# Two full sets of second-weight buffers, four staging buffers and no resident token operands in an attention and mixture-of-experts kernel

## The chip, the cores and the metric

The kernel runs on one core of a Trainium2 chip. The metric is the device time of one execution in microseconds, the median of several runs. Engines are named as in the profile: PE is TensorE (its weight loads are PEld), DVE is VectorE, ACT is ScalarE, POOL is GpSimd, SP is SyncE, which issues all the transfers.

## What is computed

Linear attention with positive random features feeds a dense mixture of eight experts. The reference, cut to what matters:

```python
def _attn_ref(q, k, v, omega):                 # q, k, v: (4, 8, 576, 64), omega: (128, 64)
    def phi(x):
        h = np.einsum('bhsd,md->bhsm', x, omega) - np.sum(x * x, axis=-1, keepdims=True) / 2.0
        h = h - np.max(h, axis=-1, keepdims=True)
        return np.exp(h) / np.sqrt(m)
    q_p, k_p = phi(q_s), phi(k_s)
    kv = np.einsum('bhsm,bhsd->bhmd', k_p, v)
    ...
    return num / den
def _moe_ref(x, w_gate, w1, w2):               # x: (2304, 512), w1: (8, 512, 1024), w2: (8, 1024, 512)
    P = np.exp(x @ w_gate - max); 8 times: rows normalized, columns normalized
    for e in range(E):
        out += P[:, e:e + 1] * (np.maximum(x @ w1[e], 0.0) @ w2[e])
```

`x` is the attention's output, 2304 tokens of 512 features. The output is 2304 x 512 in float32.

## The kernel before

**Stages.** The attention part and the preparation of the token operands take about the first 219 us of the profile. Then the experts run in 16 units: a unit `u` is one expert and one half of its 1024 hidden columns (`units`, L172). In a unit, tokens go in three chunks of 768 (`NCH`) for the first layer and in nine pairs of 128-token tiles (`n` from 0 to 8, `steps`, L504) for the second.

**Seven products.** Each of the two layers is cut into 2 x 2 blocks and multiplied with seven products in place of eight; `ORDER = [1, 5, 6, 3, 7, 2, 4]` (L91) is the order in which they are taken. For that, sums of blocks are made of the weights (`split`, L187), of the tokens (`token_operands`, L97) and of the hidden activations (`left_operands_a` and `left_operands_b`, L593 and L609). Each float32 operand is cut into a high part (a rounding copy on ACT: `wh`, `ah`, `sh`, `bh`) and a low part (a subtraction on DVE: `wl`, `al`, `sl`, `bl`), and each product is high x high, high x low and low x high, so six matmuls of 256 columns in the second layer and two times six of 384 columns in the first.

**First layer.** `first(u, c, i, g)` (L527) multiplies token operand `i` of chunk `c` (tiles `xs`, or `xr`) by first weight `i` into `hx` or `hz`; DVE and ACT gather it in `hr` and `hn`. The first layer runs one chunk ahead of the second: the list `todo` is taken up five, five and four pieces a pair.

**Second layer.** `second(s, i)` (L630) multiplies a left operand by second weight `i` in a bank `x`, `z` or `w`, and DVE adds the result, times the token's weight `prob`, to the output tile (`out`, L660). A bank takes the next product only after that eviction.

**Weights of the next unit.** `stage(u, w)` (L176) loads first (`w` = 1) or second (`w` = 2) weights in two halves into staging tiles `st`. `split(u, w, i)` makes operand `i` from them: a combining step on POOL (in place in `st`, or in `t`) for 5, 6, 7 and 4 of the second weights and for 5, 6, 3 and 7 of the first, the high part on ACT, the low part on DVE (L193, L223, L224).

- There are three staging buffers, so the second half of the second weights has to wait until a half of the first weights is used up.
- First weights have 7 buffers for each part, second weights 7 + `W2X` = 11: four products of the next unit can be made while the present set is in use. In the code they stand ahead of pairs 4 to 7; the other three follow the last uses in pair 8.

**Token operands.** The 21 operands (three chunks of seven, 768 KB each) are in DRAM (`xd`). Operand 1 of each chunk (`RES = (1,)`) is loaded once and stays in a tile `xr`. The other six of a chunk are loaded again in each unit into four rotating buffers (`XSB`); `load_next` (L513) loads the next one when an operand has been used.

**What sets the order.** The code gives an order and priorities; a scheduler then places the instructions of each engine in a queue by its own estimate of when operands and buffers are ready, and it may move an instruction far ahead of its place in the code. Each engine takes its queue strictly in order. SP's queue holds the staging loads and the token loads together, so a load there waits behind one whose buffer is not free.

```python
pool = wp if w == 1 else op_
bufs = 7 + W2X * (w == 2)
hi = pool.tile([P, 2, HD], F32R, tag=f"w{w}h", bufs=bufs, name="wh")
lo = pool.tile([P, 2, HD], F32R, tag=f"w{w}l", bufs=bufs, name="wl")
nc.scalar.copy(hi, o)
```

Of the kernel before, what the change touches and what calls it, by code (L numbers as in the profile page):

```python
# [9 lines left out]
F32 = mybir.dt.float32  # L10
# [6 lines left out]
def raw(ap):  # L17

    return ap.bitcast(F32)
# [3 lines left out]
def moe_attention_kernel(  # L23
# [29 lines left out]
    P = 128  # L53
# [3 lines left out]
    SM = JM * P  # L57
    SR = S - SM
    XSB = 4
    RES = (1,)  # L60
    W2X = 4
    FB = 4
    NFB = FF // P // FB
    CT = 6
# [3 lines left out]
    HD = DM // 2  # L68
# [5 lines left out]
    wp = ctx.enter_context(tc.tile_pool(name="wp", bufs=1, side="right"))  # L74
# [14 lines left out]


    ORDER = [1, 5, 6, 3, 7, 2, 4]  # L91
    xdram = {}

    def token_tile():
# [2 lines left out]
    def token_operands(c, x):  # L97
# [11 lines left out]

        for i in ORDER:  # L110
            if i == 5:
# [61 lines left out]
    wst, wt = {}, {}  # L173
    tmp = {}

    def stage(u, w):  # L176
        e, fb = units[u]
        f0 = fb * FB * P
        for r in range(2):
            wst[u, w, r] = t = wp.tile([P, 2, 2, HD], F32, tag="st", bufs=3, name="st")  # L180
            if w == 1:
                src = w1[e][r * HD : (r + 1) * HD, f0 : f0 + FB * P]
            else:
                src = w2[e][f0 + r * HD : f0 + (r + 1) * HD, :]
            nc.sync.dma_start(out=t.rearrange("p k h c -> p k (h c)"), in_=src.rearrange("(k p) c -> p k c", p=P))

    def split(u, w, i):  # L187

        def q(r, h):
            return wst[u, w, r][:, :, 1 - h if w == 1 else h]  # L190

        def tt(o, a, b, op=ALU.subtract):
            nc.gpsimd.tensor_tensor(o, a, b, op=op)  # L193


        if w == 1:

            if i == 5:
                tmp[u] = wp.tile([P, 2, HD], F32, tag="t", bufs=1, name="t")
                tt(tmp[u], q(0, 1), q(1, 1), ALU.add)  # L200
            elif i == 6:
                tt(tmp[u], tmp[u], q(0, 0))
            elif i == 3:
                tt(tmp[u], q(1, 0), tmp[u])
            elif i == 7:
                tt(q(0, 1), q(0, 0), q(0, 1))
            o = {1: q(0, 0), 7: q(0, 1), 2: q(1, 0), 4: q(1, 1)}[i] if i not in (5, 6, 3) else tmp[u]
        else:

            if i == 5:  # L210
                tt(q(0, 0), q(0, 1), q(0, 0))
            elif i == 6:
                tt(q(0, 0), q(0, 0), q(1, 1))
            elif i == 7:
                tt(q(0, 1), q(1, 1), q(0, 1))
            elif i == 4:
                tt(q(0, 0), q(1, 0), q(0, 0), ALU.add)
            o = {3: q(1, 1), 7: q(0, 1), 2: q(1, 0)}.get(i, q(0, 0))
        pool = wp if w == 1 else op_
        bufs = 7 + W2X * (w == 2)  # L220
        hi = pool.tile([P, 2, HD], F32R, tag=f"w{w}h", bufs=bufs, name="wh")
        lo = pool.tile([P, 2, HD], F32R, tag=f"w{w}l", bufs=bufs, name="wl")
        nc.scalar.copy(hi, o)  # L223
        (nc.vector if u > 0 or (w == 2 and i in (1, 6, 7, 4)) else nc.gpsimd).tensor_tensor(lo, o, raw(hi), op=ALU.subtract)  # L224
        wt[u, w, i] = (hi, lo)
# [18 lines left out]
    for i in range(2):  # L244
        r, cl = slice(i * D, (i + 1) * D), slice(i * M, (i + 1) * M)
# [257 lines left out]
    NP = CT // 2 * NCH  # L503
    steps = [(u, n) for u in range(len(units)) for n in range(NP)]  # L504
    def order(u):

        return [NCH - 1] + list(range(NCH - 1)) if u == 0 else list(range(NCH))

    chunks = [(u, c) for u in range(len(units)) for c in order(u)]
    hraw, hneg, ops, xop, xres, hacc = {}, {}, {}, {}, {}, {}  # L510
    loads = [(u, c, i) for u, c in chunks[1:] for i in ORDER]

    def load_next():  # L513

        while loads:
            u, c, i = loads.pop(0)
            if i in RES:
                if (c, i) not in xres:
                    xres[c, i] = op_.tile([P, 2, 2, HL], F32R, name=f"xr{c}_{i}")
                    nc.sync.dma_start(out=raw(xres[c, i]), in_=xdram[c, i])  # L520
                xop[u, c, i] = xres[c, i]
                continue
            xop[u, c, i] = token_tile()
            nc.sync.dma_start(out=raw(xop[u, c, i]), in_=xdram[c, i])
            return

    def first(u, c, i, g):  # L527
# [38 lines left out]
        if g == 1 or both is None:  # L566
# [5 lines left out]
            else:  # L572
                nc.scalar.copy(o, src)  # L573
        if g == 1 and (u, c) != chunks[0] and i not in RES:
            load_next()

    def tiles_of(u, n):

        c, j = order(u)[n // (CT // 2)], n % (CT // 2)
        return [CT * c + j, CT * c + j + CT // 2]  # L580
# [81 lines left out]
    def store(t):  # L662
        b, j = t // JM, t % JM
        if b < B:
            dst = out[b * S : b * S + SM, :].rearrange("(p j) d -> p j d", j=JM)[:, j, :]
            nc.sync.dma_start(out=dst, in_=outt[t])
        else:
            for a in range(2):
                r0 = (2 * j + a) * S + SM
                nc.sync.dma_start(out=out[r0 : r0 + SR, :], in_=outt[t][a * SR : (a + 1) * SR, :])  # L670

    pieces = [(u, c, i, g) for u, c in chunks for i in ORDER for g in range(2)]

# [56 lines left out]
    for i, jb in enumerate(jobs):  # L730
# [4 lines left out]
        if i >= 8 and i % 2 == 0 and (i - 8) // 2 < 7:  # L735
            split(0, 1, ORDER[(i - 8) // 2])
        if i == 24:
# [20 lines left out]
    for _ in range(XSB):  # L758
        load_next()
    for i in ORDER:  # L760
        split(0, 2, i)
# [3 lines left out]
    for s, (u, n) in enumerate(steps):  # L765
        c = n // (CT // 2)
        more = u + 1 < len(units)
        if u == NFB:
            for t in tiles_of(u, n):
                nc.vector.tensor_scalar_mul(outt[t], outt[t], prob[:, t, 0:1])  # L770
        if more:
            if n == 1:
                stage(u + 1, 1)
            if n == 2:
                split(u + 1, 1, ORDER[0])
            if n == NP - 2 - W2X:
                stage(u + 1, 2)
            if NP - 1 - W2X <= n < NP - 1:
                split(u + 1, 2, ORDER[n - (NP - 1 - W2X)])
        for k, i in enumerate(ORDER):  # L780
            second(s, i)
            if n == NP - 1 and more and k + W2X < len(ORDER):
                split(u + 1, 2, ORDER[k + W2X])
            if k < (5, 5, 4)[n % 3] and todo:
                pc = todo.pop(0)
                first(*pc)
                j = ORDER.index(pc[2])
                if pc[1] == order(pc[0])[-1] and pc[3] == 1 and pc[0] + 1 < len(units) and j + 1 < len(ORDER):
                    split(pc[0] + 1, 1, ORDER[j + 1])
            if i == 7 and s + 1 < len(steps):  # L790
                left_operands_a(s + 1)
            if k in (1, 4):
                next(gate, None)
        if s + 1 < len(steps):
            left_operands_b(s + 1)
        if s == NFB * NP - 1:
            for _ in gate:
                pass
        if u == len(units) - 1:
            for t in tiles_of(u, n):  # L800
                store(t)
        ops.pop(s)
# [28 lines left out]
```

## Time and profile before

| | |
|---|---|
| median of 3 runs | 1668.83 us (1668.63 to 1671.46) |
| profiled execution | 1676.44 us, span 1674.7 us |
| PE busy | 1626.8 us, 97% |
| PEld busy | 1601.4 us, 96% |
| DVE busy | 1430.5 us, 85% |
| ACT busy | 783.6 us, 47% |
| POOL busy | 250.1 us, 15% |
| DMA | 293.19 MB in the main queue, 53.0% of 16 engines |

A profile is one execution seen by engine. Busy time is the union of an engine's instructions. Matmuls are pipelined and overlap in the list, so the distance from one start to the next says what a matmul costs when nothing holds it. "Idle before" is the time in which an engine did nothing, and the arrow names what ended it. The chain of waits is followed back from the last instruction, at each step to what released it.

### The profile page before, as it was taken

To read this page: it belongs to the slowest core of one execution; us is meant where nothing else is said; L and a number is where in the kernel's file an instruction comes from. 1 tells how busy PE (TensorE), PEld (TensorE's weight loads), DVE (VectorE), ACT (ScalarE), POOL (GpSimd) and SP (SyncE) were. 2 spreads that over 40 slices of the span, in tenths; PEclk is the share of its full clock that TensorE was granted. 3 is DMA by queue.
4 is the path that set the end of the run, shared out by engine and by line. 5 is a ranking of instruction groups with operands and counts; after the bars stand their busy time and mean duration, and the time that the engine had idled before them with its cause. 6 is when DMAs were issued, how large, how long until landed. Compare 5 with 4: busy or idle time off the path is not lost.

```text
span 1674.7 us, 29917 instructions
## 1 busy us (share of the span) xinstructions
PE 1626.8 (97%) x11610; PEld 1601.4 (96%) x11610; DVE 1430.5 (85%) x2903; ACT 783.6 (47%) x1408; POOL 250.1 (15%) x232
## 2 busy tenths in 40 slices
PE   7999989999999999999999999999999999999998
PEld 7899889999999999999999999999999999999997
DVE  7999788898978888898888887888889888888878
ACT  6777645443344344443444443434444344444432
POOL 7531131110111011010101010101101010101000
PEclk9999999999999999999999999999999999999999
DMA  9422575554554555556555454555564654555452
GB/s 242 119 80 99 218 284 190 196 194 159 169 177 159 195 175 176 195 162 209 177 175 188 163 187 163 176 189 183 166 206 157 205 185 162 189 159 194 159 189 76
DMA packets 96347, 295.08 MB, mean 176 GB/s; under 512 B 13776, under 2 KB 38352, under 8 KB 96208
## 3 DMA queue, kind: packets, MB, share of 16 engines
q1 hardware_dynamic: 96208, 293.19, 53.0%
q8 instruction: 92, 1.51, 0.4%
q14 instruction: 47, 0.39, 0.1%
HBM read 271.93 MB, written 21.23 MB: 175 GB/s over the span
## 4 chain that ended last, share of the span: by engine, by line
PE 73%; DVE 16%; DMA 5%; issue 2%; ACT 2%; POOL 1%; SPq 0%; ACTq 0%; DVEq 0%
PE hx L554 20%; PE x L640 19%; PE hz L554 13%; PE z L640 10%; DMA st<-in_moe_w_dram 5%; PE w L640 5%; DVE sm L591 3%; DVE wl L224 2%; DVE out L660 2%; DVE hr L571 1%; PE np L433 1%; DVE mx L347 1%; POOL st L193 1%; ACT wh L223 1%; DVE bl L591 1%
## 5 line engine op out<-in xcount | busy, mean ns | idle before, releaser
L554 PE MATMUL hx<-xs,wh 128*128 128x384 f32 x1160 | 279.9, 336 | 0.8 <-ACT hr L573 0.5
L554 PE MATMUL hz<-xs,wh 128*128 128x384 f32 x1152 | 278.3, 336 | 0.0
L660 DVE SCALAR_TENSOR_TENSOR out<-x,prob,out 128x256 f32<-128x256 f32 x504 | 237.8, 476 | 22.9 <-PE x L640 22.8
L554 PEld LDWEIGHTS hx<-xs,wh 128*128 128x128 f32 x1160 | 204.1, 188 | 1.4 <-ACT hr L573 0.9
L554 PEld LDWEIGHTS hz<-xs,wh 128*128 128x128 f32 x1152 | 203.2, 188 | 0.1
L622 ACT ACTIVATE bh<-hr 128x512 fp32r<-128x512 f32 x144 | 91.1, 633 | 233.0 <-PE x L640 188.1
L223 ACT CAST wh<-st 128x512 fp32r<-128x512 f32 x176 | 106.7, 618 | 194.9 <-POOL st L193 80.1
L224 DVE TENSOR_TENSOR wl<-st,wh 128x512 fp32r<-128x512 f32 x169 | 135.1, 802 | 67.2 <-ACT wh L223 66.3
L660 DVE SCALAR_TENSOR_TENSOR out<-z,prob,out 128x256 f32<-128x256 f32 x252 | 120.1, 476 | 83.2 <-PE z L640 83.0
L591 DVE SCALAR_TENSOR_TENSOR sm<-hr,sm 128x256 f32<-128x256 f32 x288 | 147.8, 513 | 3.9
L554 PE MATMUL hx<-xs,wl 128*128 128x384 f32 x580 | 150.8, 336 | 0.0
L554 PE MATMUL hz<-xs,wl 128*128 128x384 f32 x576 | 149.7, 335 | 0.0
L193 POOL TENSOR_TENSOR st<-st 128x512 f32<-128x512 f32 x80 | 106.7, 1342 | 231.1 <-DMA st<-in_moe_w_dram 177.0
L618 ACT CAST sh<-sm 128x512 fp32r<-128x512 f32 x144 | 89.6, 622 | 99.7 <-PE z L640 75.6
L640 PE MATMUL z<-wh,sh 128*128 128x256 f32 x576 | 117.4, 284 | 13.0 <-DVE out L660 12.2
L640 PE MATMUL x<-wh,sh 128*128 128x256 f32 x576 | 118.9, 288 | 2.7 <-ACT wh L223 1.3
L640 PE MATMUL z<-wl,sh 128*128 128x256 f32 x576 | 119.6, 282 | 0.8 <-POOL wl L224 0.8
L640 PE MATMUL x<-wl,sh 128*128 128x256 f32 x576 | 117.0, 281 | 0.0
L640 PE MATMUL z<-wh,sl 128*128 128x256 f32 x576 | 115.1, 281 | 1.8 <-DVE sl L606 1.8
L640 PE MATMUL x<-wh,sl 128*128 128x256 f32 x576 | 115.4, 281 | 0.0
L591 DVE SCALAR_TENSOR_TENSOR bl<-hr,bh 128x512 fp32r<-128x512 f32 x144 | 112.9, 784 | 0.0
L193 POOL TENSOR_TENSOR t<-st 128x512 f32<-128x512 f32 x16 | 21.2, 1322 | 608.4 <-DMA st<-in_moe_w_dram 527.3
(153 smaller groups left out, 3968.4 us busy)
## 6 DMA issues: line engine op xcount, KB each, us to landing
xs<-xd SPq DMA_DIRECT2D x282, 768.0 KB, 4.4
st<-in_moe_w_dram SPq DMA_DIRECT2D x64, 512.0 KB, 5.7
xd<-xs SPq DMA_DIRECT2D x21, 768.0 KB, 4.2
k<-in_k_dram SPq DMA_DIRECT2D x8, 512.0 KB, 6.7
v<-in_v_dram SPq DMA_DIRECT2D x8, 512.0 KB, 5.6
q<-in_q_dram SPq DMA_DIRECT2D x8, 512.0 KB, 6.5
out_dram<-out SPq DMA_DIRECT2D x16, 256.0 KB, 2.3
xr<-xd SPq DMA_DIRECT2D x3, 768.0 KB, 11.5
```

What stands on the lines that cost most here:

```text
L193: nc.gpsimd.tensor_tensor(o, a, b, op=op)
L223: nc.scalar.copy(hi, o)
L224: (nc.vector if u > 0 or (w == 2 and i in (1, 6, 7, 4)) else nc.gpsimd).tensor_tensor(lo, o, raw(hi), op=ALU.subtract)
L347: nc.vector.reduce_max(mx, p3, axis=AX.X)
L433: nc.tensor.matmul(n3[:, i, :], lhsT=qt[g][:, i, :], rhs=kvs[key[0]][:, h, :], start=True, stop=True)
L554: nc.tensor.matmul(pb, lhsT=a[:, k, g * P : (g + 1) * P], rhs=x[:, b, k, :], start=i in (1, 5, 2) and j == 0, stop=j == len(prods) - 1, sk ...
L571: nc.vector.tensor_tensor(o, src, o, op=ALU.add)
L591: nc.vector.scalar_tensor_tensor(o, in0=a, scalar=0.0, in1=b, op0=ALU.max, op1=op)
L618: nc.scalar.copy(sh, sm)
L622: nc.scalar.activation(bh, a[:, 1:], AF.Relu)
L640: nc.tensor.matmul(pb, lhsT=ops[s][i][a][:, f], rhs=wt[u, 2, i][b][:, f], start=bool(start) and j == 0, stop=j == len(prods) - 1, skip_gro ...
L660: nc.vector.scalar_tensor_tensor(o, in0=pb, scalar=prob[:, t, e : e + 1], in1=o, op0=ALU.mult, op1=ALU.add)
```

## The change

```diff
-    RES = (1,)
-    W2X = 4
+    RES = ()
...
+    W2AT = [(5, 2), (6, 0), (6, 3), (7, 0), (7, 3), (8, 0), (8, 3)]
...
-            wst[u, w, r] = t = wp.tile([P, 2, 2, HD], F32, tag="st", bufs=3, name="st")
+            wst[u, w, r] = t = wp.tile([P, 2, 2, HD], F32, tag="st", bufs=4, name="st")
...
-        bufs = 7 + W2X * (w == 2)
+        bufs = 7 * w
...
-            if n == NP - 2 - W2X:
+            if n == 2:
                 stage(u + 1, 2)
-            if NP - 1 - W2X <= n < NP - 1:
-                split(u + 1, 2, ORDER[n - (NP - 1 - W2X)])
         for k, i in enumerate(ORDER):
             second(s, i)
-            if n == NP - 1 and more and k + W2X < len(ORDER):
-                split(u + 1, 2, ORDER[k + W2X])
+            if more and (n, k) in W2AT:
+                split(u + 1, 2, ORDER[W2AT.index((n, k))])
```

- Second weights have 14 buffers for each part, two full sets.
- Staging has four buffers. The second weights are staged in pair 2 of the code and not in pair 3.
- The seven splits of the second weights stand at seven places in pairs 5 to 8 (`W2AT`), behind product `k` of pair `n`.
- No token operand is resident: operand 1 of each chunk goes through the four rotating buffers too, so seven of seven are loaded in each unit.

In the changed kernel's listing, line numbers are one higher from L92 on to the changed loop.

**SP's queue in unit 9, pairs 4 to 7, before.** `xs` is a token load, its source `xd0_5` is operand 5 of chunk 0; `st_13184` is the second half of the second weights of unit 10.

```order
L524 DMA xs_13361<-xd0_5_1826 128x1536
L524 DMA xs_13395<-xd0_6_1908 128x1536
L185 DMA st_13184<-in_moe_w2_dram 128x2x512
L524 DMA xs_13472<-xd0_3_1986 128x1536
L524 DMA xs_13507<-xd0_7_2076 128x1536
```

The same place in the changed kernel; `st_14189` and `st_14191` are the two halves of the second weights of unit 11:

```order
L525 DMA xs_13409<-xd0_1_1733 128x1536
L525 DMA xs_13443<-xd0_5_1826 128x1536
L186 DMA st_14189<-in_moe_w2_dram 128x2x512
L525 DMA xs_13515<-xd0_6_1908 128x1536
L525 DMA xs_13554<-xd0_3_1986 128x1536
L186 DMA st_14191<-in_moe_w2_dram 128x2x512
L525 DMA xs_13635<-xd0_7_2076 128x1536
```

The staging of second weights stands one unit further ahead, and operand 1 of chunk 0 (`xd0_1`) is loaded like the others.

**DVE's queue where unit 9 ends and unit 10 begins, before.** `wl` is a low part of a weight, here of second weights of unit 10; `out` rows are evictions, `sm`, `al`, `bl`, `sl` belong to the left operands.

```order
L660 SCALAR_TENSOR_TENSOR out14_3431<-x_13783,prob_79,out14_3431 128x256
L591 SCALAR_TENSOR_TENSOR al_13868<-hr_13566,ah_13867 128x256
L224 TENSOR_TENSOR wl_13793<-st_13182,wh_13792 128x512
L591 SCALAR_TENSOR_TENSOR sm_13892<-hr_13566,sm_13871 128x256
L591 SCALAR_TENSOR_TENSOR sm_13892<-hr_13566,sm_13892 128x256
L660 SCALAR_TENSOR_TENSOR out16_3300<-x_13671,prob_79,out16_3300 128x256
L660 SCALAR_TENSOR_TENSOR out17_3432<-z_13803,prob_79,out17_3432 128x256
L591 SCALAR_TENSOR_TENSOR bl_13780<-hr_13195,bh_13779 128x512
L224 TENSOR_TENSOR wl_13812<-st_13184,wh_13811 128x512
L660 SCALAR_TENSOR_TENSOR out14_3431<-x_13783,prob_79,out14_3431 128x256
L224 TENSOR_TENSOR wl_13833<-st_13182,wh_13832 128x512
```

The changed kernel, some ten instructions later in the queue; the `wl` rows are four of the seven second weights of unit 11:

```order
L607 TENSOR_TENSOR sl_13927<-sm_13925,sh_13926 128x512
L592 SCALAR_TENSOR_TENSOR sm_14037<-hr_13613,hn_13885 128x512
L225 TENSOR_TENSOR wl_14723<-st_14189,wh_14722 128x512
L225 TENSOR_TENSOR wl_14793<-st_14191,wh_14792 128x512
L225 TENSOR_TENSOR wl_14844<-st_14189,wh_14843 128x512
L592 SCALAR_TENSOR_TENSOR sm_14058<-hr_13613,sm_14037 128x256
L225 TENSOR_TENSOR wl_14914<-st_14191,wh_14913 128x512
L592 SCALAR_TENSOR_TENSOR sm_14058<-hr_13613,sm_14058 128x256
L661 SCALAR_TENSOR_TENSOR out17_3434<-x_13842,prob_79,out17_3434 128x256
```

Three low parts, needed in the next pair, have given way to a run of four that are needed a unit later; of the other three, one stands in pair 7, one in pair 8 and one a few rows further on.

**PE's queue where the second layer begins, before** (`x_3170<-...,ah` is the first product; `hz_3212` belongs to operand 5 of the next chunk):

```order
L554 MATMUL hz_3067<-xs_3043,wl_1203 128x384 x2
L554 MATMUL hz_3067<-xs_3043,wh_1202 128x384 x2
L640 MATMUL x_3170<-wh_3138,ah_3096 128x256 x2
L640 MATMUL x_3170<-wl_3139,ah_3096 128x256 x2
L640 MATMUL x_3170<-wh_3138,al_3097 128x256 x2
L554 MATMUL hz_3212<-xs_3130,wh_639 128x384 x2
```

and in the changed kernel:

```order
L555 MATMUL hz_3067<-xs_3043,wl_1203 128x384 x2
L555 MATMUL hz_3067<-xs_3043,wh_1202 128x384 x2
L555 MATMUL hx_3178<-xs_3128,wh_515 128x384 x2
L555 MATMUL hx_3178<-xs_3128,wl_516 128x384 x2
L555 MATMUL hx_3178<-xs_3128,wh_515 128x384 x4
L555 MATMUL hx_3178<-xs_3128,wl_516 128x384 x2
L555 MATMUL hx_3178<-xs_3128,wh_515 128x384 x2
L641 MATMUL x_3168<-wh_3136,ah_3096 128x256 x2
```

The twelve matmuls of operand 1 of the next chunk, which used the resident tile and stood behind the first four products, now stand ahead of all of them.

## Rows read from the trace of the kernel before

**Rows 1.** The page, busy us (share of the span) and instructions.

```profile
PE 1626.8 (97%) x11610; PEld 1601.4 (96%) x11610; DVE 1430.5 (85%) x2903; ACT 783.6 (47%) x1408; POOL 250.1 (15%) x232
```

**Rows 2.** Busy time by stretch: length, then PE, PEld, DVE, ACT, POOL, clock, DMA.

```profile
594.00:1503.00 909.00, 896.16 (x6305) 888.61 (x6304) 778.80 (x1492) 391.27 (x650) 104.34 (x80) 1.00 0.55 180
...
318.00:594.00 276.00, 271.33 (x1889) 266.88 (x1889) 239.19 (x471) 117.74 (x196) 33.87 (x24) 1.00 0.53 178
...
220.00:230.00 10.00, 6.15 (x28) 5.43 (x27) 9.93 (x13) 5.20 (x11) 5.92 (x5) 0.84 1.02 420
```

**Rows 3.** The chain of waits, 780 to 885 us: start, us, what, how many.

```profile
784.70 2.08 PE hx L554 x12
...
800.64 2.10 PE hx L554 x12
...
803.55 0.71 PE x L640 x6
...
811.93 0.35 DVE sm L591
...
818.49 6.43 DMA st<-in_moe_w_dram
```

**Rows 4.** Waits, 594 to 1503 us: us in total, times, longest.

```profile
PE z L640 <- DVE out L660: 11.0, 10, 1.3
...
DVE wl L224 <- ACT wh L223: 51.6, 30, 3.7
```

**Rows 5.** VectorE's instructions in order of time: start, us, what [idle before].

```profile
820.57 0.41 DVE L591 SCALAR_TENSOR_TENSOR al<-hr,ah 128x256 fp32r<-128x256 f32 x1
...
822.10 0.95 DVE L571 TENSOR_TENSOR hr<-hz,hr 128x768 f32<-128x768 f32 x1
822.97 0.68 DVE L224 TENSOR_TENSOR wl<-st,wh 128x512 fp32r<-128x512 f32 x1
823.57 0.42 DVE L591 SCALAR_TENSOR_TENSOR sm<-hr,sm 128x256 f32<-128x256 f32 x1
826.95 1.12 DVE L224 TENSOR_TENSOR wl<-st,wh 128x512 fp32r<-128x512 f32 x1 [2.97 <-ACT wh L223]
828.00 0.47 DVE L660 SCALAR_TENSOR_TENSOR out<-x,prob,out 128x256 f32<-128x256 f32 x1
828.39 1.33 DVE L591 SCALAR_TENSOR_TENSOR sm<-hr,sm 128x256 f32<-128x256 f32 x1
```

**Rows 6.** GpSimd's instruction at that time.

```profile
828.15 1.29 POOL L193 TENSOR_TENSOR st<-st 128x512 f32<-128x512 f32 x1 [0.63 <-DVE wl L224]
```

**Rows 7.** TensorE's instructions after pauses, and one at the start of unit 0.

```profile
225.31 0.50 PE L640 MATMUL z<-wh,sl 128*128 128x256 f32 x2 [1.79 <-DVE sl L606]
227.09 0.79 PE L640 MATMUL x<-wh,sh 128*128 128x256 f32 x2 [1.28 <-ACT wh L223]
...
229.48 1.15 PE L554 MATMUL hx<-xr,wh 128*128 128x384 f32 x4
...
830.78 0.50 PE L640 MATMUL z<-wh,sh 128*128 128x256 f32 x2 [1.28 <-DVE out L660]
```

**Rows 8.** The main DMA queue; landing of token loads, then of staging, 594 to 1503.

```profile
q1 hardware_dynamic: 96208, 293.19, 53.0%
...
DMA to landing us min/median/max: 4.0/4.4/7.1
...
DMA to landing us min/median/max: 3.6/5.7/7.2
```

**Rows 9.** Groups of VectorE instructions: count, busy us, mean ns, idle before.

```profile
L224 DVE TENSOR_TENSOR wl<-st,wh 128x512 fp32r<-128x512 f32 x169 | 135.1, 802 | 67.2 <-ACT wh L223 66.3
...
L591 DVE SCALAR_TENSOR_TENSOR sm<-hr,sm 128x256 f32<-128x256 f32 x288 | 147.8, 513 | 3.9
...
L591 DVE SCALAR_TENSOR_TENSOR bl<-hr,bh 128x512 fp32r<-128x512 f32 x144 | 112.9, 784 | 0.0
```

**Rows 10.** The waits of SyncE's queue: us in total, times, longest.

```profile
SPq L185 <- DVE wl L224: 96.3, 40, 10.3
```

## The prediction

> **What bounds the kernel now.** The busy shares come first: TensorE works in 97% of the span [rows 1], so only its pauses can be won. The next view, busy time by stretch, shows where they are. From 219 us on sixteen units follow, each one half of one expert. The stretch 594:1503 holds 6305 matmuls, which is 10.0 units of 630 [rows 2].
>
> A unit's floor comes from the chain of waits: a block of twelve first-layer matmuls takes 2.08 to 2.10 us where nothing holds it, a block of six second-layer ones 0.71 us [rows 3]. A unit has 21 blocks of twelve and 63 of six: 21 x 2.09 + 63 x 0.71 = 88.6 us. Ten units are 886 us and the stretch is 909, so about 22 us, **2.2 us a unit**, are lost. That is all that this change can touch there.
>
> What ends last in a unit? The list of waits for TensorE in that stretch has one large entry: a z product waits for VectorE's eviction, ten times, 11.0 us [rows 4]. The chain shows what lies behind it: a second-weight transfer is issued at 818.49, when the low part of a first weight has freed its staging buffer, and takes 6.43 us [rows 3]. GpSimd combines, ScalarE makes the high part, and VectorE, whose next instruction in order is the low part (wl), has stood idle 2.97 us at 826.95 [rows 5]. All behind it on VectorE is late, and TensorE pauses 1.28 us at 830.78 [rows 7]. VectorE has three such waits a unit, 51.6 us in ten units, 5.2 us a unit [rows 4]; the long ones belong to the two halves of the second weights, neither of which is ready when VectorE comes to it.
>
> **The change part by part.** *Four staging buffers.* In the order printed for the changed kernel, the two halves of a unit's second weights stand in SyncE's queue in pairs 4 and 5 of the unit two ahead of their use, and the first low part made from them stands on VectorE in pair 7. Two pairs lie between, some 20 us at 909/90 = 10.1 us a pair; a staging transfer lands in 5.7 us, at most 7.2 [rows 8]. So nearly all of VectorE's 5.2 us of idle a unit goes.
>
> *Two full sets.* The seven products are not spread as the code writes them. The order puts each low part right behind the last use of the set two units older, so one stands in pair 7, one in pair 8 and five close together around the first pair of the next unit. TensorE needs none of them for another unit, but they are on VectorE's path. Between its evictions of product 1 of pair 0 and of pair 1 of unit 10 VectorE now has 7 evictions at 0.39, 9 subtractions and sums of 512 columns at 0.60 (five of them the low parts), one al at 0.41, two sums of 256 columns at 0.35 and two first-layer sums at 0.87, start to start [rows 3, 5]: 11.0 us. TensorE has 36 first and 42 second matmuls there: 3 x 2.09 + 7 x 0.71 = 11.2. That is the densest pair, and tight by itself.
>
> GpSimd's combining steps come on top. A 256-column sum takes 0.42 us alone and 1.33 beside one; an eviction beside one stays at 0.47 [rows 5, 6]. The excess of the groups' means over the undisturbed time is (802 - 680) x 169 + (513 - 420) x 288 + (784 - 680) x 144 ns = 62 us over 128 combining steps, 0.49 us each [rows 5, 9]. Three of a unit's four second-weight steps fall in that pair, 1.5 us: VectorE needs 12.5 against 11.2 and is 1.3 us over.
>
> What does being over cost? By the same count, pairs 3 and 4 of the old order give VectorE 19.2 + 5 x 0.49 + 2.97 idle = 24.6 against 22.4 of TensorE: 2.2 over, for a pause of 1.28 [rows 7]. So some 0.9 are absorbed, and 1.3 over costs 0.4. The bounds are 0 (pairs 7 and 8 have 2 us of slack each, by the count) and 1.3 (nothing absorbed). I take 0.6, nearer to the count but above it, since the new order repeats only every five units and its densest pair differs. Of the unit's other losses (2.2 less 1.3) I keep 0.4; the rest I put down to the other idle of VectorE. A unit goes **from 2.2 to 1.0 us** of loss; for units 4 to 14, 11 x 1.2 = **13 us**.
>
> *Units 1 to 3.* The stretch 318:594 holds 1889 matmuls, 3.0 units, 265.7 us at the floor: 10 us lost [rows 2], part of it behind the same transfers, part behind the normalization of `prob` and the scaling of `out` on VectorE, which stay. I take **4 us** (bounds 0 and 7).
>
> *All token operands streamed.* Three loads go and 47 come: 44 more issues of 768 KB, 34 MB on 293, and the DMA share of 53% goes to about 59% [rows 8]. No engine computes more. The cover is the distance from the last use of the operand four places back: in the new order at least 24 first and 18 second matmuls, 2 x 2.09 + 3 x 0.71 = 6.3 us, where it was 36 and 30, 9.8 us. A load lands in 4.4 us, at most 7.1 [rows 8]. Some fifteen loads have less than 8 us of cover; the middle one has 14. I cost it at nothing; the bounds are 0 and 7.1 - 6.3 = 0.8 us for each of the fifteen.
>
> *Start of unit 0.* The first operand of the second chunk was a resident tile in a pool that opens late, and its twelve matmuls stand behind four products that wait: TensorE idles 1.79 and 1.28 us there [rows 7], and the granted clock of 220:230 is 0.84, so partly at 1.2 GHz after those pauses [rows 2]. Now these twelve stand ahead of the first product, where VectorE (9.93 of 10 us busy, [rows 2]) holds TensorE anyway: 2.1 us of matmuls go into idle time, and they leave the slow clock, at which four of them took 1.15 us [rows 7]. I take **3 us** (1 to 4).
>
> **Sum.** 13 + 4 + 3 = 20 us. The profiled execution took 1676.4 us (span 1674.7 and 1.7 around it), 0.5% above the median of 1668.8. 20 in 1676 is 1.2%, and 1668.8 x 0.988 = **1649 us**.
>
> **The rivals.** *All of it comes back:* the bunch is absorbed and units run near the floor, 0.3 lost: 11 x 1.9 + 7 + 4 = 32 us, 1637. For it: three low parts already stand behind released buffers in a unit's last pair, and the waits show nothing for them [rows 4]. Against it: there are five now, in a tight pair.
>
> *The bunch takes the place of the wait:* VectorE's overrun at each unit's start costs what the late transfer cost, 2 us. Then only the 3 us of unit 0 and little of units 1 to 3 remain: 1664 to 1668. For it: the 11.0 against 11.2 above. Against it: 5.2 us of idle are returned to the same engine.
>
> *GpSimd holds VectorE for its whole step:* at 1.29 us for each of the three [rows 6] the pair is 3.7 over, 2.8 us of pause and 0.4 elsewhere: 3.2 a unit, 11 us more over eleven units, 7 us less elsewhere, 1673. For it: the 1.33 us row. Against it: the mean of 0.49. The Trainium skill, page "SBUF — State Buffer", section "Who interferes with whom", has this as its rule: a VectorE instruction with two SBUF inputs and a GpSimd one that reads SBUF shut each other out, whichever starts first for its whole length. The 1.33 us row agrees with it; most meetings here are shorter.
>
> *Token loads late (slower):* a load behind a staging transfer in SyncE's queue leaves only when a low part has freed a buffer: 40 such waits, 2.4 us on average, 10.3 at most [rows 10]. If that falls on a load with 6.3 us of cover and the longest landing, TensorE waits 2.4 + 7.1 - 6.3 = 3.2 us; once in each of 15 units that is 48 us less the 20: 1697, and in half of the units 1673. It decides where wait and landing together pass the cover. Against it: the loads right behind a staging transfer have 7 us and more, most of them 13 to 16.
>
> *It doesn't do what it says:* the places named in the new table don't set where the products stand; the release of buffers does. That is in the forecast.
>
> **How the numbers follow.** The forecast (1642 to 1658) 0.55; all comes back (below 1642) 0.13; part of it lost to the bunch (1658 to 1665.5) 0.10; the bunch takes it all (1665.5 to 1669) 0.08; GpSimd holds in full (1669 to 1675) 0.05, of which 0.01 slower; token loads late 0.09. A measurement of this kernel can tell about 0.2%, 3.3 us, from no change. Faster: 0.55 + 0.13 + 0.10 = 0.78; within 0.2%: 0.12; slower: 0.10. Below 1638 I leave 0.07 and above 1668 0.13, so the range is 1638 to 1668.
>
> **What would show it.** Right: in ten units VectorE's waits for wh fall from 51.6 us to under 15; the z wait of 1.3 us is gone; small waits for evictions appear around the first pair of a unit; a unit takes 89 to 90 us; no first matmul waits for a token transfer; the clock at the start of unit 0 is 1.00. Wrong: TensorE pauses of over 1 us at each unit's start, or waits of hx or hz for DMA.

## The result, and the profile after

The changed kernel takes 1656.3 us, the median of six runs (1652.3 to 1658.2), beside 1671.7 for the kernel before (1668.6 to 1673.6, six runs, the three shown first among them). The ratio is 0.9906, 95% interval 0.9895 to 0.9917: **15 us faster**. In a second set of runs (e10 below) the two stood at 1656.2 and 1674.3, ratio 0.9895 (0.9876 to 0.9915). The forecast was 1.2%, 1649 us; the range 1638 to 1668 holds the time.

Three lines of the page of after: busy time, the main DMA queue (packets, MB, share), and the chain that ended last; below them the chain of before.

```profile
PE 1617.2 (98%) x11610; PEld 1598.3 (97%) x11610; DVE 1430.6 (87%) x2903; ACT 785.4 (48%) x1408; POOL 276.4 (17%) x232
q1 hardware_dynamic: 102544, 327.79, 58.1%
PE 87%; DVE 11%; ACT 1%; issue 1%; SPq 0%; DMA 0%; POOL 0%; ACTq 0%; DVEq 0%
...
PE 73%; DVE 16%; DMA 5%; issue 2%; ACT 2%; POOL 1%; SPq 0%; ACTq 0%; DVEq 0%
```

VectorE has the same work as before [rows 1], and GpSimd's 232 instructions take 26 us longer. The DMA share is 58.1%, where 59% was worked out. Transfers were 5% of the chain and are 0% now.

Busy time by stretch, columns as in [rows 2]: length, PE, PEld, DVE, ACT, POOL, clock, DMA.

```profile
590.00:1486.00 896.00, 892.96 (x6309) 888.71 (x6308) 781.63 (x1494) 394.09 (x654) 126.75 (x80) 1.00 0.60 209
318.00:590.00 272.00, 269.49 (x1896) 267.18 (x1895) 238.97 (x471) 118.20 (x197) 37.63 (x24) 1.00 0.60 206
220.00:230.00 10.00, 7.59 (x37) 7.38 (x38) 8.10 (x12) 5.10 (x11) 6.03 (x5) 0.83 0.53 201
```

The first stretch holds 6309 matmuls, 10.01 units of 630 matmuls each; at the floor of 88.6 us that is 887.2, so 8.8 us are lost, **0.9 a unit** where it was 2.2. The second holds 3.01 units, 266.6 us, and 5.4 are lost where it was 10.

The waits of 590 to 1486 us (total, times, longest):

```profile
DVE out L661 <- PE x L641: 41.3, 52, 2.8
DVE out L661 <- PE z L641: 41.3, 38, 3.3
DVE wl L225 <- ACT wh L224: 7.6, 10, 1.3
PE w L641 <- DVE bl L592: 1.7, 6, 0.4
PE w L641 <- DVE out L661: 0.8, 2, 0.4
PE x L641 <- DVE out L661: 0.4, 2, 0.2
```

VectorE's wait for wh is 7.6 us where it was 51.6, and TensorE's wait of the z product, 11.0 us before, is gone [rows 4]. VectorE now waits for TensorE.

To compare kernels I took one sum from every trace: the distance of each matmul of the sixteen units from the start of the one before it, less 0.117 us in the second layer and 0.174 in the first (0.71 over 6 and 2.09 over 12, [rows 3]), and of this all that is over 0.03 us. It is called the loss; what the three columns on the right do not hold lies in unit 15 (4.2 to 5.0 us) and ahead of the first second-layer product. Second-layer starts in these profiles lie between 215.8 and 223.2 us, at 217.9 and 219.9 in two of one kernel; the loss leaves that out. It also leaves out the distance behind a matmul of another line. One of these holds a pause, in the first pair of unit 0 behind the matmul of L472 (L473 in the changed kernel). To have it in, add to the loss and to unit 0 0.9 us for before and e9, 1.2 for the changed kernel, e1, e2, e3 and e6, 1.9 for e5, e11 and e12, and nothing for e4, e7 and e8.

| kernel | second-weight, staging, token buffers | ratio to before | loss, us | unit 0 | units 1-3 | units 4-14 |
|---|---|---|---|---|---|---|
| before | 11, 3, 4 + 3 resident | 1 | 48.4 | 7.1 | 10.6 | 25.0 |
| changed | 14, 4, 4 | 0.9906 | 25.6 | 5.5 | 5.7 | 9.4 |
| e1 | 11, 3, 4 | 1.0004 | 43.2 | 6.8 | 9.8 | 20.4 |
| e2 | 11, 4, 4 | 0.9927 | 30.5 | 5.7 | 6.1 | 13.0 |
| e3 | 14, 3, 4 | 1.0151 | 64.9 | 6.8 | 9.4 | 42.9 |
| e9 | 10, 4, 4 + 3 resident | 0.9932 | 31.3 | 7.0 | 6.5 | 11.8 |
| e4 | 14, 4, 3 | 0.9925 | 30.5 | 5.9 | 11.8 | 7.2 |
| e8 | 14, 5, 3 | 0.9905 | 31.5 | 5.2 | 16.1 | 4.5 |
| e7 | 13, 4, 5 | 0.9931 | 35.6 | 4.9 | 5.8 | 19.2 |
| e6 | 14, 4, 4, sums on VectorE | 0.9882 | 25.8 | 4.9 | 4.6 | 10.7 |
| e5, e11 | 14, 4, 4, unit 0 on VectorE | 0.9876, 0.9886 | 24.5, 23.1 | 3.1, 1.7 | 5.9, 6.2 | 9.6, 9.6 |
| e12 | e6 and e5 together | 0.9874 | 24.8 | 3.5 | 4.3 | 10.9 |

### The profile page after: what moved, and what is told of

Same layout as the page of the kernel before. It is cut to its first block, busy times and chain, and to the rows that moved or that the text cites. A ratio compares the mean times of both kernels' runs of the same rounds, so it can differ in the third digit from the quotient of the medians.

```text
span 1650.6 us, 30079 instructions
## 1 busy us (share of the span) xinstructions
PE 1617.2 (98%) x11610; PEld 1598.3 (97%) x11610; DVE 1430.6 (87%) x2903; ACT 785.4 (48%) x1408; POOL 276.4 (17%) x232
## 3 DMA queue, kind: packets, MB, share of 16 engines
q1 hardware_dynamic: 102544, 327.79, 58.1%
## 4 chain that ended last, share of the span: by engine, by line
PE 87%; DVE 11%; ACT 1%; issue 1%; SPq 0%; DMA 0%; POOL 0%; ACTq 0%; DVEq 0%
PE hx L555 24%; PE x L641 22%; PE hz L555 18%; PE z L641 11%; PE w L641 6%; DVE out L661 2%; DVE sm L592 1%; PE np L434 1%; DVE bl L592 1%; DVE mx L348 1%; PE kv L364 1%; PE qp L411 1%; DVE sl L620 1%; DVE cn L351 1%; PE pp L342 1%; DVE wl L225 1%
## 5 line engine op out<-in xcount | busy, mean ns | idle before, releaser
L555 PE MATMUL hx<-xs,wh 128*128 128x384 f32 x1536 | 371.9, 336 | 0.4 <-DVE prob L162 0.3
L555 PE MATMUL hz<-xs,wh 128*128 128x384 f32 x1152 | 282.0, 337 | 0.0
L555 PEld LDWEIGHTS hx<-xs,wh 128*128 128x128 f32 x1536 | 269.1, 188 | 0.8 <-issue 0.5
L194 POOL TENSOR_TENSOR st<-st 128x512 f32<-128x512 f32 x80 | 132.1, 1652 | 710.5 <-DVE wl L225 705.8
L555 PE MATMUL hx<-xs,wl 128*128 128x384 f32 x768 | 199.6, 336 | 0.0
L592 DVE SCALAR_TENSOR_TENSOR sm<-hr,sm 128x256 f32<-128x256 f32 x288 | 137.4, 477 | 2.6
L555 PEld LDWEIGHTS hx<-xs,wl 128*128 128x128 f32 x768 | 138.7, 188 | 0.0
L225 DVE TENSOR_TENSOR wl<-st,wh 128x512 fp32r<-128x512 f32 x169 | 121.8, 732 | 8.0 <-ACT wh L224 7.7
L592 DVE SCALAR_TENSOR_TENSOR bl<-hr,bh 128x512 fp32r<-128x512 f32 x144 | 118.3, 822 | 3.4 <-ACT bh L623 3.4
L600 ACT ACTIVATE ah<-hr 128x256 fp32r<-128x256 f32 x144 | 60.4, 419 | 119.2 <-PE x L641 94.5
```

The source lines that it names most:

```text
L555: nc.tensor.matmul(pb, lhsT=a[:, k, g * P : (g + 1) * P], rhs=x[:, b, k, :], start=i in (1, 5, 2) and j == 0, stop=j == len(prods) - 1, sk ...
L592: nc.vector.scalar_tensor_tensor(o, in0=a, scalar=0.0, in1=b, op0=ALU.max, op1=op)
L600: nc.scalar.activation(ah, a11, AF.Relu)
```

## The experiments

### Which part brings it: e1, e2, e3 and e9

The theory was that the fourth staging buffer takes a transfer off VectorE's path; the rivals were the two full sets and the streaming. Three kernels made from the kernel before (e1, e2, e9) and one from the changed kernel (e3) set them apart.

**e1**, streaming alone:

```diff
-    RES = (1,)
+    RES = ()
```

> The kernel before with one edit: no resident token operand, all streamed (three staging buffers, eleven second-weight buffers as before). Theory (the fourth staging buffer brings the gain): VectorE's waits for wh stay at about 5 us a unit and one z wait of about 1.3 us a unit stays; only the matmuls at the start of unit 0 move, 1.6 us. Ratio to before 0.998 to 1.000. Rival A (streaming frees the path, it brings most of the gain): ratio 0.991 to 0.994. Rival B (token loads come late): ratio above 1.003, and waits of hx or hz for DMA in the trace.

1672.2 us beside 1671.7, ratio 1.0004 (0.9994 to 1.0014). 34 MB more are moved and nothing is paid or won. The two waits stay, the z wait at 0.65 us a unit and not at the 1.3 expected:

```profile
DVE wl L224 <- ACT wh L223: 44.2, 27, 3.7
...
PE z L640 <- DVE out L660: 6.5, 10, 1.3
```

**e2**, streaming and the fourth staging buffer:

```diff
-    RES = (1,)
+    RES = ()
...
-            wst[u, w, r] = t = wp.tile([P, 2, 2, HD], F32, tag="st", bufs=3, name="st")
+            wst[u, w, r] = t = wp.tile([P, 2, 2, HD], F32, tag="st", bufs=4, name="st")
```

> The kernel before with two edits: all token operands streamed, and a fourth staging buffer; eleven second-weight buffers and their old places. Theory (staging buffer): VectorE's waits for wh in ten units fall from 51.6 us to under 15 and the z waits of 1.3 us go, without the two full sets; ratio to before 0.990 to 0.993, within 0.2% of the full change. Rival (the two full sets bring it, the transfer then has a unit more in which to land): ratio 0.997 to 1.000, waits stay.

1659.2 us, ratio 0.9927 (0.9914 to 0.9940). One buffer of 512 KB more and the z waits are gone; of the waits for wh this is left, a little more than expected:

```profile
DVE wl L224 <- ACT wh L223: 18.9, 20, 2.7
```

**e3**, the changed kernel without its fourth staging buffer, that is, streaming and two full sets:

```diff
-            wst[u, w, r] = t = wp.tile([P, 2, 2, HD], F32, tag="st", bufs=4, name="st")
+            wst[u, w, r] = t = wp.tile([P, 2, 2, HD], F32, tag="st", bufs=3, name="st")
```

> The changed kernel with three staging buffers in place of four: two full sets of second weights and streaming stay. Theory (staging buffer): the second half of the second weights still waits for a buffer and then lands in 4 to 8 us; in the queue the low parts behind it stand in pair 4 of a unit, so VectorE's waits for wh stay above 30 us in ten units, and TensorE's pauses behind them above 0.8 us a unit; ratio to before 0.995 to 0.999. Rival (two full sets bring it: nothing of the set is needed in the same unit, so a late one costs nothing): ratio 0.990 to 0.993.

1696.4 us, ratio **1.0151** (1.0134 to 1.0168): slower than before by 25 us, which neither side expected, and with only 21.8 us of waits for wh, where I had put more than 30. So the length of VectorE's wait doesn't set the cost; what stands behind it does. The chain of waits in unit 6 (start, us, what):

```profile
822.74 5.53 DMA st<-in_moe_w_dram
...
828.34 1.30 POOL st L194
...
829.66 0.63 ACT wh L224
...
831.83 1.53 DVE wl L225
833.36 0.79 DVE out L661 x2
834.14 0.60 DVE sl L620
834.74 0.40 DVE out L661
835.14 0.60 DVE sl L607
835.74 1.20 DVE wl L225 x2
...
837.88 0.60 DVE wl L225
838.48 0.41 DVE out L661
```

and TensorE's instructions after pauses at the same place:

```profile
833.81 0.51 PE L641 MATMUL x<-wh,bh 128*128 128x256 f32 x2 [0.30 <-DVE out L661]
835.19 0.50 PE L641 MATMUL x<-wh,sh 128*128 128x256 f32 x2 [0.41 <-DVE out L661]
838.93 0.51 PE L641 MATMUL x<-wh,ah 128*128 128x256 f32 x2 [2.05 <-DVE out L661]
```

With room for a whole set, five low parts stand close together in VectorE's queue in pairs 4 and 5, behind the late half. When it lands, the evictions that TensorE needs are spread between them, and TensorE pauses 2.8 us in 5 us. Of the 42.9 us lost in units 4 to 14, 38 lie in pairs 4 to 6, nearly all of it in pair 5. This is the prediction's rival "the bunch takes the place of the wait", and it is real where the bunch stands behind a transfer.

**e9**, the fourth staging buffer alone, with the resident operands of before; the room comes from the second weights, 10 buffers in place of 11:

```diff
-    W2X = 4
+    W2X = 3
...
-            wst[u, w, r] = t = wp.tile([P, 2, 2, HD], F32, tag="st", bufs=3, name="st")
+            wst[u, w, r] = t = wp.tile([P, 2, 2, HD], F32, tag="st", bufs=4, name="st")
```

> The kernel before with its resident token operands and a fourth staging buffer; the room for it comes from the second weights, 10 buffers for each part in place of 11. Theory (the fourth staging buffer alone brings most of the gain, streaming was only the price of the room): VectorE's waits for wh in ten units fall from 51.6 to under 20 us, and the ratio to before is 0.991 to 0.995. Rival (it takes the streamed operands, or 11 buffers and more, besides): 0.997 or above.

1663.2 us beside 1674.3, ratio 0.9932 (0.9919 to 0.9946), and the wait for wh is

```profile
DVE wl L224 <- ACT wh L223: 10.9, 18, 1.8
```

The fourth staging buffer brings 0.7% with eleven buffers and streaming or with ten and resident operands. On top of it, the two full sets and the streamed operands bring some 0.2 to 0.4% (0.9906 against 0.9927, each to before in its own set of runs, and 0.9895 against 0.9932 in one set); without it, two full sets cost 1.5%. The earlier staging (pair 2 for pair 3) and the new places of the splits came with the two full sets; no run parts them.

### Are the token loads near the path: e4, e7 and e8

**e4**, three rotating token buffers, `XSB = 4` to `XSB = 3` in the changed kernel:

> The changed kernel with three rotating token buffers in place of four. By the queues the least time between the last use of the operand three places back and the first use of the new one falls from 6.3 to 4.7 us at full pace, and 53 of 326 loads have under 7 us where 13 of 325 had. Theory (a load lands in 4.4 us, and waits of SyncE's queue are short beside that): a handful of loads a unit come a little late, ratio to the changed kernel 1.000 to 1.006, sum of hx and hz waits for DMA under 10 us. Rival (token loads late, the price of streaming is near): 3 loads a unit late by 2 to 3 us each, ratio to the changed kernel 1.05 or more.

1658.1 us, ratio to before 0.9925 (0.9908 to 0.9943), 0.2% over the changed kernel. From unit 4 on less is lost than with four buffers, though the cover is a quarter shorter. Operands come late by 7.0 us in all, 4.7 of it between 215 and 590 us (first line) and 2.3 from 590 us on (second line):

```profile
PE hz L555 <- DMA xs<-xd: 4.7, 6, 1.7
...
PE hx L555 <- DMA xs<-xd: 2.3, 3, 1.5
```

In the changed kernel and in e1, with four buffers, TensorE has no wait for a token load in the whole execution.

**e7**, five token buffers and, for the room, 13 buffers for second weights:

```diff
-    XSB = 4
+    XSB = 5
...
-        bufs = 7 * w
+        bufs = 7 * w - 1 * (w == 2)
```

> The changed kernel with five rotating token buffers (the least cover grows from 6.3 to 11.2 us by the queues) and, to make room, 13 buffers for each part of the second weights. Theory (token loads are hidden with four already): ratio to the changed kernel 0.999 to 1.001. Rival (what is left of the loss, 25.6 us, hangs on the token loads): ratio 0.996 or less. If 14 buffers rather than 13 matter, ratio above 1.001.

1664.9 us, ratio to before 0.9931 (0.9916 to 0.9946). Nearly twice the cover wins nothing, and the changed kernel has no wait for a token load to win, so the loads aren't the limit. By the ratios to before and by the loss, 35.6 us against 25.6, the kernel is slower than the changed one, as in the third case of the expectation; but two things were changed, and no run shows which of them makes the queues worse. Of the 19.2 us lost in units 4 to 14, 18.6 lie in pairs 1 and 2. VectorE is busy 23 us longer with the same instructions:

```profile
PE 1620.1 (98%) x11610; PEld 1597.6 (96%) x11610; DVE 1453.7 (88%) x2903; ACT 782.2 (47%) x1408; POOL 264.8 (16%) x232
```

That alone isn't the reason: in e4 and e8 it is busy 1457.0 and 1458.9 us, and they lose the least in units 4 to 14. At one of the new pauses a 256-column sum takes 1.34 us beside a GpSimd step of a *first* weight, and a z product waits 0.67 us behind it:

```profile
1065.85 1.34 DVE L592 SCALAR_TENSOR_TENSOR sm<-hr,sm 128x256 f32<-128x256 f32 x1
...
1067.64 0.50 PE L641 MATMUL z<-wh,sh 128*128 128x256 f32 x2 [0.67 <-DVE out L661]
```

**e8**, three token buffers and a fifth staging buffer (`XSB = 3`, `bufs=5` for `st`):

> The changed kernel with three rotating token buffers and, in the room that this gives, a fifth staging buffer. Theory (four staging buffers already take the transfer off the path): the same as with three token buffers and four staging buffers, ratio to the changed kernel 1.000 to 1.002. Rival (SyncE's queue still waits for staging buffers, 102 us in ten units, and this hurts): ratio 0.995 to 0.998, and SyncE's waits for wl under 30 us in ten units.

1660.8 us, ratio to before 0.9905 (0.9889 to 0.9921; the changed kernel has 0.9906 and 0.9895 in other sets of runs). The 102 us of SyncE's waits for low parts in the expectation are those of the whole execution; from 590 to 1486 us the changed kernel has 74.5, e4 70.6 and e8 70.0. So the fifth buffer leaves these waits where they were, and this run can't say what they cost. Nothing is gained over four: units 4 to 14 are at 4.5 us, the least of all kernels here, and units 1 to 3 give it back (16.1), where 7.3 us of waits for token loads lie between 215 and 590 us. By the table, a kernel with the queues of e8 from unit 4 on and those of the changed kernel before would be some 5 us faster (9.4 less 4.5, an estimate); no edit here does that.

### What GpSimd costs VectorE: e6

The four combining steps of the second weights of units 1 to 15 on VectorE:

```diff
         def tt(o, a, b, op=ALU.subtract):
-            nc.gpsimd.tensor_tensor(o, a, b, op=op)
+            (nc.vector if w == 2 and u > 0 else nc.gpsimd).tensor_tensor(o, a, b, op=op)
```

> The changed kernel with the four combining steps of the second weights of units 1 to 15 (60 of 128 in all) on VectorE in place of GpSimd. Theory (a GpSimd step costs VectorE 0.5 us on average): VectorE takes 0.60 us for each step and is spared 0.5, so its work in a unit grows by 0.4 us, it gets the steps into the dense first pair, and ratio to the changed kernel is 1.000 to 1.004. Rival (GpSimd holds VectorE for its whole step of 1.3 us): VectorE is spared 0.7 us a step, 2.8 us a unit, its busy time falls by some 40 us and the ratio is 0.995 to 0.998.

1656.7 us, ratio to before 0.9882 (0.9865 to 0.9899), against 0.9906 and 0.9895 of the changed kernel in other sets of runs: the same, as far as sets can be compared.

```profile
PE 1622.1 (98%) x11610; PEld 1602.8 (97%) x11610; DVE 1432.4 (87%) x2963; ACT 782.8 (47%) x1408; POOL 178.6 (11%) x172
```

VectorE has 60 instructions more and its busy time grows by 1.8 us, not by 36 (60 at 0.60) and not down by 40: by this a step on GpSimd costs VectorE about 0.57 us, (36 - 1.8) / 60, nearly what the step costs on VectorE itself. That is an estimate and takes the rest of VectorE's work as unchanged; the order of the queues alone moves it, the same 2903 instructions taking 1410.0 us in e2 and 1458.9 in e8. The prediction's mean of 0.49 agrees with it, and the fall of 40 us that the rival of 1.3 us a step asked for did not come.

### The start of unit 0: e5, e10, e11 and e12

**e5** and, on the chip of e10, **e11**: unit 0's last three low parts from GpSimd to VectorE.

```diff
-        (nc.vector if u > 0 or (w == 2 and i in (1, 6, 7, 4)) else nc.gpsimd).tensor_tensor(lo, o, raw(hi), op=ALU.subtract)
+        (nc.vector if u > 0 or w == 2 else nc.gpsimd).tensor_tensor(lo, o, raw(hi), op=ALU.subtract)
```

> The changed kernel with the three low parts of unit 0's second weights that GpSimd makes (5, 3 and 2) made by VectorE. Theory (GpSimd stretches VectorE at the start of unit 0): in the changed kernel TensorE pauses 0.52, 1.04 and 1.46 us around the product 5 of the first pair, while GpSimd's low part takes 1.57 us and VectorE's bl, sm and sl take 1.78, 1.48 and 1.75 us where 0.68, 0.42 and 0.68 is what they take alone; without it the three pauses together fall from 3.0 to 2.0 us or less. Rival (VectorE's own work is the bound there): they stay within 0.3 us of 3.0 or grow. Ratio to the changed kernel 0.999 to 1.001 either way; the trace decides.

> The kernel with unit 0's second-weight low parts on VectorE once more, beside the changed kernel on one chip. If what the trace showed at the start of unit 0 (2.4 us less lost there, 1.4 us of it in other places given back) is all, the ratio to the changed kernel is 0.998 to 1.000; if the 0.3% between their ratios to before is real, 0.996 to 0.998.

TensorE after its pauses at that place in the changed kernel:

```profile
219.31 0.50 PE L641 MATMUL z<-wh,sh 128*128 128x256 f32 x2 [0.52 <-ACT wh L224]
...
220.96 0.50 PE L641 MATMUL z<-wl,sh 128*128 128x256 f32 x2 [1.04 <-POOL wl L225]
222.92 0.50 PE L641 MATMUL z<-wh,sl 128*128 128x256 f32 x2 [1.46 <-DVE sl L607]
...
224.06 1.48 PE L555 MATMUL hz<-xs,wh 128*128 128x384 f32 x4
```

and in e5:

```profile
222.51 0.50 PE L641 MATMUL z<-wh,sh 128*128 128x256 f32 x2 [0.53 <-ACT wh L224]
...
224.91 0.80 PE L641 MATMUL z<-wl,sh 128*128 128x256 f32 x2 [1.79 <-DVE wl L225]
...
227.21 1.28 PE L555 MATMUL hz<-xs,wh 128*128 128x384 f32 x4
```

The three pauses of 3.0 us become two of 2.3. I had put 2.0 or less, so the theory is right in sign and too large; the low part on VectorE stands behind three others there. Ratios to before are 0.9876 (0.9861 to 0.9891) and 0.9886 (0.9872 to 0.9900). Beside the changed kernel on one chip it is 1655.7 against 1656.2 us, within what can be told. With the pause that the table leaves out, unit 0 loses 5.0 us in e5 and 6.7 in the changed kernel, 1.7 less and not the 2.4 of e11's expectation; and 3.1 us are lost in the last pair of unit 1, where the changed kernel loses 1.4.

**e10** is the changed kernel for this comparison.

> The changed kernel once more, beside the others of this call, to compare them on one chip. Ratio to before 0.989 to 0.992.

1656.2 us beside 1674.3, ratio 0.9895 (0.9876 to 0.9915); its loss is 25.6 us, as in its first profile.

**e12**, both edits:

> Both of the last two edits in the changed kernel: unit 0's second-weight low parts and the combining steps of units 1 to 15 on VectorE. By the sums of losses that each showed alone, the start of unit 0 at 3 us in place of 5.5 and the rest unchanged: ratio to the changed kernel 0.997 to 1.000, the fastest of these. Rival (the queues that the scheduler makes from it put other products late, as in units 1 to 3): 1.000 to 1.003.

1653.6 us, ratio to before 0.9874 (0.9855 to 0.9892). It is the fastest median, 0.16% under e10 on the same chip, but the intervals overlap, and its loss, with the pause that the table leaves out, is 0.1 us less (26.7 against 26.8). That it beats the changed kernel isn't shown.

## Why the prediction was right, and where it wasn't

**Four staging buffers: right.** The chain read ahead of the change (transfer, GpSimd, high part, low part, eviction, z product) was the one to cut. Waits for wh went from 51.6 us to 7.6, under the 15 named, and the z wait went. e2 and e9 show that this buffer alone brings 0.7%.

**Two full sets: the size was right, the place and the reason were not.** I put VectorE at 12.5 us against TensorE's 11.2 in the first pair of a unit, and a pause of 0.6. VectorE is full there, and TensorE doesn't pause: over units 4 to 14 the first pairs lose 0.5 us together, where 0.6 a unit was put. Around the start of unit 10 (its first product stands at 1127.9; columns as above):

```profile
1122.00:1133.50 11.50, 11.50 (x81) 11.33 (x80) 11.43 (x23) 6.65 (x12) 5.34 (x3) 1.00 0.52 176
```

The count without GpSimd, 11.0 us, was good: from 1128 to 1139 us VectorE is busy 10.93. The 1.5 us on top were not paid in that pair. Here is VectorE:

```profile
1124.87 0.95 DVE L592 SCALAR_TENSOR_TENSOR al<-hr,ah 128x256 fp32r<-128x256 f32 x1
...
1128.34 1.88 DVE L225 TENSOR_TENSOR wl<-st,wh 128x512 fp32r<-128x512 f32 x3
1130.14 0.41 DVE L592 SCALAR_TENSOR_TENSOR sm<-hr,sm 128x256 f32<-128x256 f32 x1
1130.48 0.68 DVE L225 TENSOR_TENSOR wl<-st,wh 128x512 fp32r<-128x512 f32 x1
...
1131.42 0.47 DVE L661 SCALAR_TENSOR_TENSOR out<-x,prob,out 128x256 f32<-128x256 f32 x1
```

and GpSimd:

```profile
1119.38 3.11 POOL L194 TENSOR_TENSOR st<-st 128x512 f32<-128x512 f32 x2 [43.30 <-DVE wl L225]
1124.24 1.30 POOL L194 TENSOR_TENSOR st<-st 128x512 f32<-128x512 f32 x1 [1.75 <-DVE wl L225]
1129.10 3.55 POOL L194 TENSOR_TENSOR st<-st 128x512 f32<-128x512 f32 x1 [3.56 <-DVE wl L225]
```

The prediction put three of the four steps into that pair; three of them run ahead of it, in pair 8. The step at 1124.24 holds `al` for 0.5 us. The last, started while VectorE was in a run of low parts, takes 3.55 us in place of 1.3, and the low parts take 0.60 each, as if it weren't there: in this dense run it is GpSimd that is held. The loss sits elsewhere, in pairs 2 and 8, with 3.9 and 4.8 of the 9.4 us of units 4 to 14. There a combining step meets a `bl`, an `sl` or a sum behind which a product or an eviction waits (in unit 7, `bl` at 942.29 takes 1.78 us beside GpSimd's step):

```profile
944.12 0.50 PE L641 MATMUL w<-wh,bl 128*128 128x256 f32 x2 [0.35 <-DVE bl L592]
```

Pair 2 lost 4.1 us before the change too, beside steps of first weights: that is the 0.4 us a unit that I kept, 0.35 measured. What the two full sets brought is pair 8, 0.44 us a unit, where nothing was lost before. So my 1.0 us a unit came out at 0.9 by luck in part: one of its two terms, 0.6 in the first pair, stood in the wrong place and for the wrong reason, and another of about its size took its place. e3 shows what the bunch costs with a wait ahead of it. So the prediction's rival with the bunch hangs on the transfer, which the prediction treated apart.

The Trainium skill, page "SBUF — State Buffer", section "Who interferes with whom", says that the two engines, where VectorE reads two inputs from SBUF and GpSimd reads SBUF too, shut each other out, whichever comes first. The trace agrees in both directions, 0.95 us for `al` and 3.55 for GpSimd's step; the prediction had used it in one direction only.

**Units 4 to 14, 13 us; units 1 to 3, 4 us.** By the stretches above it is 11 x 1.35 = 14.9 and 4.9; by the loss 15.6 and 4.9. Both are more than I put, and yet the median moved less than 20 us. The two profiles differ by 24.0 us (1676.4 and 1652.4), the medians by 15.3 and 18.0; the profile of after lies 3.9 us under its own median. The step that was mis-sized is the first: 2.2 us a unit was read from one profiled execution, which, at 1676.4 us, lies 4.7 over the median of 1671.7. The prediction scaled that away as a share of the whole. e1 takes as long as the kernel before, has the same waits, and its profile, of a run at its median (1672.4), has 4.9 us less loss (pause of unit 0 counted), 4.6 of it in units 4 to 14: its z waits are 6.5 us in ten units and not 11.0. Measured from e1, units 4 to 14 gain 11.0 us, 1.0 a unit. That the kernel before loses about as much in a usual run is argued, not shown: it has one profile only, and why its z waits were longer there stays open.

**Streaming: right.** e1 gives 1.0004, and with four buffers no matmul waits for a token load. With three, e4, loads begin to come late, most of them in units 0 to 3; with five, e7, nothing is won.

**The start of unit 0, 3 us: mis-sized, and one sign of it wrong.** With the pause that the table leaves out, unit 0's loss fell from 8.0 to 6.7, by 1.3. The twelve matmuls do stand ahead of the first product, and its wait of 0.77 us for VectorE is gone. But I had counted two pauses behind it, 1.79 and 1.28 us [rows 7], and there were three; this one stood ahead of them, behind GpSimd's low part (kernel before):

```profile
223.02 0.50 PE L640 MATMUL z<-wl,sh 128*128 128x256 f32 x2 [0.78 <-POOL wl L224]
```

The three are 0.52, 1.04 and 1.46 us now, 3.0 in place of 3.9; one stands behind GpSimd's low part and one behind `sl`, stretched to 1.75 us. The granted clock of 220:230 is 0.83 where I had said 1.00, and now most of the twelve matmuls of the next operand stand at the slow level, four of them in 1.48 us. What I overlooked is that the matmuls moved forward leave the next ones to stand behind the pauses.

**The rivals.** "All of it comes back" asked for 0.3 us a unit; e8 has that in units 5 to 14, so a loss that small can be reached, though not by this change. "Doesn't do what it says" is so in part: with seven quite different places in `W2AT` each engine's queue comes out with the same operations on the same tiles in the same order. The release of buffers sets where the products stand, as the forecast had it; there is no run of such a kernel.

## What to carry to other kernels

Before making room for work further ahead, look for the transfer that the present work waits for: one staging buffer for that brought 0.7%, while two full sets of operands without it made an in-order engine carry a late transfer and five steps behind it, and cost 1.5%. An overlap that fills one engine isn't a cost by itself; it costs where a result that another engine waits for stands behind something late. And a sum worked out from one profiled execution should be held against the spread of the runs: here that execution lay 4.7 us over the median, and the forecast, 20 us, was 4.7 over the gain of 15.3.

## What was not expected of the hardware

- **The clock after the same pauses.** e5 and e11 are one kernel, on two chips. In both, TensorE pauses 0.53 and 1.79 us at the start of unit 0. In e5 the granted clock of 220:230 is 0.83, so partly at 1.2 GHz, and four matmuls of 384 columns take 1.28 us; in e11 it is 1.00, 2.4 GHz throughout, and they take 0.85, and unit 0 loses 1.4 us less. So whether the clock falls there isn't set by the kernel alone. The two, e5 first:

```profile
220.00:230.00 10.00, 7.69 (x40) 7.18 (x39) 9.96 (x14) 6.85 (x13) 5.40 (x4) 0.83 0.63 238
```

```profile
220.00:230.00 10.00, 7.69 (x48) 7.12 (x47) 9.86 (x15) 6.18 (x13) 4.73 (x4) 1.00 0.78 287
```

- **GpSimd held by VectorE.** With the low parts in runs, the mean of GpSimd's combining step in staging tiles went from 1.34 us (106.7 us for 80) to 1.65, its longest 3.83, while VectorE's low parts fell from 802 ns [rows 9] to 732. The longest steps were held not for one instruction but for a whole run of them: the one at 1129.10 ends 1.23 us after VectorE turns to evictions at 1131.42, and two others (3.82 and 3.83 us, at 859.74 and 948.85) end 1.23 and 1.24 us after VectorE's first instruction with an input from a matmul's bank, at 862.33 and 951.44. The groups of after, and GpSimd's of before (busy us, mean ns, idle before):

```profile
L194 POOL TENSOR_TENSOR st<-st 128x512 f32<-128x512 f32 x80 | 132.1, 1652 | 710.5 <-DVE wl L225 705.8
...
L225 DVE TENSOR_TENSOR wl<-st,wh 128x512 fp32r<-128x512 f32 x169 | 121.8, 732 | 8.0 <-ACT wh L224 7.7
...
L193 POOL TENSOR_TENSOR st<-st 128x512 f32<-128x512 f32 x80 | 106.7, 1342 | 231.1 <-DMA st<-in_moe_w_dram 177.0 <-DVE wl L224 52.8
```
